# Pooled attention with a gated convolution layer: narrower waits for the second product, one operation for the values' low parts, a new written order

## The chip, the cores and the metric

The kernel runs on one core of one Trainium2 chip. The metric is the device time of one execution in microseconds (us), as the median of several runs. The engines of a core are named as the profile names them: PE is TensorE (PEld its weight loads), DVE is VectorE, ACT is ScalarE, POOL is GpSimd, SP is SyncE, which issues the DMAs here. They run side by side and wait for each other by semaphores.

## The reference, cut to what matters

```python
# q, k, v: (4 batches, 8 heads, 1152, 64) float32
q_pool = q.reshape(B, H, S // 2, 2, D).mean(axis=3)          # 576 queries
scores = np.matmul(q_pool, k.transpose(0, 1, 3, 2)) / np.sqrt(D)
scores = scores - np.max(scores, axis=-1, keepdims=True)
attn = np.exp(scores)
attn = attn / (np.sum(attn, axis=-1, keepdims=True) + 1e-09)
x = np.matmul(attn, v)        # -> (4, 576, 512), heads side by side
h = np.maximum(x @ w_in, 0.0)                                # 512 -> 1024
conv_out = sum(conv_w[k] * hp[:, k:k + S, :] for k in range(3))   # along the tokens
gate = 1.0 / (1.0 + np.exp(-conv_out))
out = (h * gate) @ w_out                                     # 1024 -> 512
```

The weights come as float64 and are turned to float32 in the kernel.

## The kernel before, in words

The program is a list of tasks, each a few instructions on one engine. The functions `loads`, `softmax`, `values`, `scales`, `feed`, `second`, `weights`, `split`, `split_out` and `halves` add 2485 tasks to a `Plan`, with an engine, a planned duration, the tasks that must come before (`after`), and the buffers that it takes and uses. A search made elsewhere has written down its result as three strings: ORDER (the order in which all tasks are emitted), SLOTS (which buffer of its ring each task takes) and SWAPPED (which tasks run on their other engine). `order()` unpacks them; the last loop of the kernel emits the tasks one by one. Every engine works through its own instructions strictly in that order, and a wait arises wherever an instruction touches a buffer that another engine or a DMA still writes or reads.

The 32 heads are worked in 16 pairs. For each pair `loads` brings keys, queries and values in, sums the two query halves and, where a head's values are split, makes a high and a low fp16 part (`hi_v`, and `lo_v` at L408, one VectorE operation for each head). `softmax` goes over five tiles of 128 queries (the last has 64 of each head): scores on PE (L468) into one of two score buffers, the maximum on VectorE (L481), the exponential on ScalarE (L486), the row totals (L499 or L503) and their inverse (L509), then either a high and a low fp16 part (L529 or L534, then L537) and a DMA transpose, or for the heads in the set X32 a normalisation (L570 or L574), transposes on PE (L588) and their eviction (L597 or L599). `values` multiplies (L620, L626) and evicts (L638 or L642, then L646 or L648 and L653).

When the four pairs of a batch have a group of query tiles ready, `feed` makes the first product in eight blocks of 128 features (L715), relu (L722 or L726), three convolution taps (L733 or L737, L744), tanh (L750) and the gate (L754). `second` then makes the second product of each of the five token tiles in four steps of two feature blocks (`mm2`: L928 for the halved groups in fp16, L934 in float32, L940 for the short last tile), evicts it (L954) and stores it (L960, L963). A tile at the end of a group needs one more column from the next group, the edge (L895, L902, L915). `weights` turns the float64 weights (L1017 to L1050); `split` and `split_out` split them into halves.

Matmuls use the array in four tile shapes: 64x128 for scores (row tiles), 64x64 for the last query tile's scores, 128x64 for values and the short token tile, and 128x128 for the rest. SP's queue issues all loads, DMA transposes and stores in the written order, too. The keys' ring has four buffers, the queries' and values' input rings have one each, the outputs' two.

Of the kernel before, what the change touches and what calls it, by code (L numbers as in the profile page):

```python
# [13 lines left out]
ALU = mybir.AluOpType  # L14
# [74 lines left out]
def unpack(words):  # L89
# [10 lines left out]
bcjykia9kekckkjzkfkdkjkaj8bGklkgbabdkzkbdQbekmbfkMbgj9kndxkokAkpd4kwd5bhkBkxkUkCbidykykDbjkHkskVkXktkNkEbkkWkq  # L100
kYkukreokFblkZlckvbmkGk0lfk1dzk9ldk2kKd8bnk3kLdLlgkIk4bwkJdBlebok5dCdDk7dElafHlhlubplbk6lxlik8d9ealjbHlrkQlklv
ebdAbsdFlylwlsbqdGbIlzdHlMbrdKkRltlplAbxlPbJlqlBlNlJlClnllbKlolOlDlQbLdRlKl4bUlElmbylFl5bulRlLlHbtl6mplSlGlTms
mqlUdSd7lIbVl1dTlVmtl7lZlWl0dVbWdWlXl8ewl2mhmrbzdXl3bXmubYbAc3lYbBdYmvbZb0mHepmwd2mEmxmImib1myl9mCmKmFbMmDmjmz
mAmcmLmJmGjjmdmMmamZmBmNdZm2memOm0d0mPmbmWmfbNm3mQmgbOmRmUm1d1mSbPd6bCm4bQnhmXkOnkmTbRmYesmlbSeunim5bTmVedm6nl
njdUb2neevjknfeteenzbvngnmnMm7nAnnb3kSnommnpb4eJkPbDefb5nwmkb6nsnNnxntnaehnbnOeinBnyncb7nunPb8nUndd3nCejnvb9nX
nDnEnVnHm8ciDInYerm9nWeLnqekDJnrelnInFemDgnZDKenocnJmnn0eqcjn1ofDhn5eZn2odnGnKjnDunLn3oeD3DiogDvckexDwoaD4clob
Dxn6ohcmn8oucneMcooxn7ovcpeNnQn9oiD5eycaojoyokgtoweODjone0oln4moozkToMD6DLnRDkoPoAcboBoNoFoCosoqDyotnSoQoroGDz
ccoIoHegoJoDooDlDnopoOomDAeznTDBDoDmDMoRe2eBo4cdDCoED7oSDNDDoTeCoKoUo5oXDPoLeDceo6oYcfppDOD8cge3pspqchDQo7oZo2
o0oVo3cqprphDpeEo8pto9pcDEo1joe4papupdD9pbpipHDqcrDFpvpKpecspweFoWpxpIDReGpfDGEapypgpJpApLeIDWEbDHpMpBctpZDSeH
DXpCDrpDeKDYEhpNpEcue5EcpOcvpSpPp0pFp2DseApGcwplp3eQcxDtp4cyDZEifjpQpzDTp1EdEepXD0Efqzp5pmp6EgpYp7pTqApVpUqaqh  # L110
DUpWqBflqfqiqdqgqCD1qbDVqepRqkqDp8qcqEeRqHECqlqjEjeSp9qmqFqIqUqJqnD2qXczqoqVqpEDqKEoqsqYqWqLqqqGqvEpq8qwEqeTqZ
eUEkficAqtq9qrqxfnEErbq0ErqyfmEFqMq1Esq5q2rcraq6Etquq3rdrmq7eVqNcBrpreEGrfrnEHrgeWEQEurjq4rqEvERrkrrEXrhrorlcC
rArsEweYrDExrBESriqQrtcDrxrurEforyrFfAeXrCrve1rOqRrzElrGrHEIEmr5rLrPEYrIrXEyrQcEr6cFrRrMe7rwsjEZrYrJE4r7fDrSJQ
skr8rNEzrTEJr9EArUsaE5gArKE0slETsmsbEnscE1EKsgsdE6snrVE2ELsee8sArWe9soshE7fEEMsffFfaENsxEBspEOEUE3EVEPE8fbsqr1
sysufCsiEWszsrfgfGpjssFifUqOsBstePe6FarZFjsvsCFbqPsDJTsOsEfcr2fdsLsFswfWsIFcsMsPsNFkE9sJr3FdffsQsKfesZsGsRFefY
sSr4fksTfZs0sHFfsWs1sUtgFgsXfqtjfXths8sYs2tis3pks4tkFhFls5s9tlr0s6tafhtuFmtmtbtntxs7trtvfrpnFAfstwtytoFVFBtpFH
# [24 lines left out]
"""
SLOTS = (
    "01232301012301231010000010101000001000000002001111111002222203000004310000111340200222650000001001100112111120"
    "02240311002005212001121411002210510300000201200113110100221230300006021100001101001101012100010110211020113010"
    "03211010011000001100011120110010012100101103110210123002101103011011021312002001011131000102102002110331110010"
    "00122201140003110001111000110013012103111020311010010202001204102013100111100201011310013210112201211010031002"
    "00011120101000301110110201233201001210001110121113140311231100201220002113312111002003211113120110031002101211"
    "10203320301212021313121000220011110023120011302101000313221103110021100110211021110321102301000012311001110100"
    "14120022100131003110200022311100101223121213102201110001031220023121110030001300111300221101220010111003223032"
    "11130000010410131220112231100103132013120102000101230302110213201211010100100211022331321001011203011210022103"  # L150
    "22301011100001202311210231130012020401113021211002000103130120010031120103001100010000202011312312130000002130"
    "31311100020001011010013120300032021011130031311111121012013000001011110000023111211132100300021030121001131011"
    "2000300301113100211001021100100110"
)
SWAPPED = """
acalaqauaDaIaMaRaVa4bdbibobsbubybGbObWb4ccckcscAcPcQcScTcUc8dadmdsdvdGeaemeseOeWe2gogygHgYhIhKhQhThXh4h6ifiBiD
iQiZi9jijjjmjnjvjxjEjNjPjRjWj5kCkEkSlilAl1l7mmmnmvmPmWm5nennnpnCnOnSn0oiokonoAoSo7pjpnpvpPpSpWp7qpqCqOqSq0q2re
rgrjrsrurGrLrRrTrZr2sgspsrsusDsRsTsWs4tatetotrtAtCtOtQt2t4t7udufulupuxuRuWu7u9vcvrvEvQvUv4v7wgwiwlwuwzwIwNwVw0
w1w5xdxfxixrxtxwxFxHxKxTxVxYx4ycygyoyqytyCyEyHySyVy9zhznzrzvzFzRzTzWz5z7AjAoAuAwACAGAKASAUAXA6BbBkBmBpByBABJBR
BVBYBZB7CcClCqCzCBCECNCYC0C6DaDeDhDiDpDwDDDJDKDRDYD5EcEiEjEqExEEELESEZFCFJFQFXF4GbGiGpGwGDGKGRGYG5HcHWH2H3H9Ia  # L160
IhIoIvIBICIJIQIXI4JbJiJwJDJMJOJYJ0J4KFKMKTK0K7LeLlLsLBLDLHLOLVL2L9MgMnMuMDMFMJMPMQMXM3M4NaNbNhNiNpNw
"""
# [11 lines left out]
def tile_pooled_attention_conv_gate_ffn(  # L174
# [11 lines left out]
    B, H, S, D = Q_SHAPE  # L186
# [56 lines left out]
    def dve(n):  # L243
        return 0.115 + n / 930.0
# [1004 lines left out]
```

## Time and profile before

| what | us |
|---|---|
| median of 3 runs | 612.47 (611.01 to 613.85) |
| the profiled execution's own time | 611.83 |
| its span in the trace | 609.9 |
| PE busy in the span | 575.6 (94%) |
| DVE busy | 567.5 (93%) |
| ACT busy | 439.5 (72%) |
| POOL busy | 297.0 (49%) |

The span runs from the first to the last instruction of the trace; the 1.9 us that the execution's own time has beyond it lie before and after. A busy share is an average over stages, so the rows further down are taken by stage. The ends of matmuls are modelled, so PE's busy time holds pauses that don't show. DMA engines were busy with the core's transfers for most of the span, 83.6% of sixteen engines' time by the packets of the one large queue.

### The profile page before, as it was taken

The page shows a single profiled execution, that of the slowest core. Times are in us where ns is not written, and L with a number is a line of the kernel's source. Part 1 is how long each engine was busy: PE and PEld are TensorE (multiplying, and loading weights), DVE is VectorE, ACT ScalarE, POOL GpSimd, SP SyncE. Part 2 cuts the span into 40 slices and gives each one's busy share as a digit, 9 for nine tenths or more (in the row PEclk, how much of TensorE's full clock was granted, in tenths as well). Part 3 has the DMA queues.
Part 4 walks back from the last instruction along what each step waited for, and adds up shares of the span by engine and source line. Part 5 has one row for each costly group of instructions (what it writes and reads, how often), then busy time and mean ns, then how long its engine had stood idle before and what let it go on. Part 6 is the DMA issues. An engine that isn't in the chain of part 4 may idle for free.

```text
span 609.9 us, 11967 instructions
## 1 busy us (share of the span) xinstructions
PE 575.6 (94%) x4454; PEld 351.7 (58%) x4454; DVE 567.5 (93%) x921; ACT 439.5 (72%) x847; POOL 297.0 (49%) x306
## 2 busy tenths in 40 slices
PE   5989998789999999999998999999999999999997
PEld 2545554466665665556566665565557456675753
DVE  4999999999999999999999999999999999999871
ACT  4999998889998977676666876567556776574431
POOL 2353545558345536436645644655363445534630
PEclk9999989999999999999999999999999999999999
DMA  8454956977958699999999599998997999898701
GB/s 295 157 194 128 216 121 157 189 164 167 231 99 228 136 170 232 203 189 176 243 186 207 141 206 191 177 227 148 222 240 139 194 202 201 146 154 149 111 35 44
DMA packets 266713, 106.97 MB, mean 175 GB/s; under 512 B 254368, under 2 KB 255648, under 8 KB 266656
## 3 DMA queue, kind: packets, MB, share of 16 engines
q1 hardware_dynamic: 266656, 106.21, 83.6%
q8 instruction: 35, 0.57, 0.4%
q14 instruction: 22, 0.18, 0.1%
HBM read 37.77 MB, written 4.72 MB: 70 GB/s over the span
## 4 chain that ended last, share of the span: by engine, by line
PE 44%; DVE 27%; issue 5%; ACT 4%; POOL 2%; DMA 1%; SPq 0%; ACTq 0%; POOLq 0%; DVEq 0%
PE s L468 11%; PE a L715 10%; DVE hl L537 9%; DVE sm L481 8%; PE a L934 7%; PE a L620 7%; DVE g L744 4%; PE a L928 3%; PE a L626 2%; PE a L588 2%; DVE g L754 1%; ACT p L486 1%; PE a L940 1%; POOL hl L529 1%; DVE v L408 1%
## 5 line engine op out<-in xcount | busy, mean ns | idle before, releaser
L486 ACT ACTIVATE p<-s,sm 128x1152 f32<-128x1152 f32 x144 | 175.3, 1219 | 64.1 <-DVE sm L481 42.0
L481 DVE TENSOR_REDUCE sm<-s 128x1 f32<-128x1152 f32 x144 | 193.1, 1347 | 11.3 <-PE s L468 9.7
L468 PE MATMUL s<-kt,qt 64*128 64x128 f32 (+2 forms) x704 | 182.4, 474 | 11.1 <-ACT p L486 6.3
L537 DVE SCALAR_TENSOR_TENSOR hl<-p,sm,hl 128x1152 f16<-128x1152 f32 (+1 forms) x111 | 161.9, 1468 | 2.7 <-POOL hl L529 1.4
L529 POOL TENSOR_SCALAR hl<-p,sm 128x1152 f16<-128x1152 f32 (+1 forms) x72 | 96.6, 1346 | 107.9 <-DVE sm L509 76.3
L468 PE MATMUL s<-kt,qd 64*128 64x512 f32 x256 | 145.4, 650 | 1.7 <-DMA kt<-in_k_dram 1.7
L620 PE MATMUL a<-pt,v 128*64 128x256 f16 (+2 forms) x1512 | 111.6, 271 | 1.3 <-ACT h L726 1.1
L468 PEld LDWEIGHTS s<-kt,qt 64*128 64x128 f32 (+1 forms) x704 | 78.6, 176 | 58.9 <-ACT p L486 24.8
L715 PE MATMUL a<-x,wi 128*128 128x257 f16 (+3 forms) x864 | 104.6, 274 | 2.4 <-ACT o L954 1.1
L620 PEld LDWEIGHTS <-v 128*64 128x64 f16 x1512 | 86.9, 110 | 20.2 <-issue 16.1
L715 PEld LDWEIGHTS <-wi 128*128 128x128 f16 x864 | 77.4, 98 | 36.7 <-issue 18.4
L737 POOL TENSOR_SCALAR g<-h,cw 128x255 f32<-128x255 f32 (+3 forms) x70 | 50.8, 730 | 61.2 <-ACT h L726 40.5
L934 PE MATMUL a<-wo,g 128*128 128x512 f32 x160 | 75.4, 605 | 0.0
L744 DVE SCALAR_TENSOR_TENSOR g<-h,cw,g 128x255 f32<-128x255 f32 (+3 forms) x144 | 73.4, 529 | 1.5 <-POOL g L737 1.1
L588 PEld LDWEIGHTS a<-ident,p 128*128 128x128 f32 (+1 forms) x360 | 37.3, 142 | 49.4 <-issue 11.9
L588 PE MATMUL a<-ident,p 128*128 128x128 f32 (+1 forms) x360 | 53.9, 278 | 12.3 <-ACT pt L597 6.5
L626 PE MATMUL a<-pt,v 128*64 128x256 f32 (+1 forms) x288 | 64.1, 408 | 0.0
L574 POOL TENSOR_SCALAR p<-p,sm 128x1152 f32<-128x1152 f32 (+1 forms) x31 | 41.6, 1344 | 44.1 <-DVE sm L509 41.2
L534 ACT ACTIVATE hl<-p,sm 128x1152 f16<-128x1152 f32 (+1 forms) x39 | 48.7, 1250 | 9.1 <-DVE sm L509 7.8
L934 PEld LDWEIGHTS a<-wo,g 128*128 128x128 f32 x160 | 28.1, 190 | 38.2 <-issue 35.9
L597 ACT ACTIVATE pt<-a 128x384 f32<-128x384 f32 (+2 forms) x100 | 45.4, 473 | 6.1 <-PE a L588 5.5
L726 ACT ACTIVATE h<-a,bs 128x257 f32<-128x257 f32 (+3 forms) x62 | 29.8, 483 | 25.6 <-PE a L715 14.3
(137 smaller groups left out, 661.9 us busy)
## 6 DMA issues: line engine op xcount, KB each, us to landing
qin<-in_q_dram SPq DMA_DIRECT2D x15, 640.0 KB, 4.7
kt<-in_k_dram SPq DMA_DIRECT2D x15, 576.0 KB, 5.1
vin<-in_v_dram SPq DMA_DIRECT2D x9, 576.0 KB, 4.6
g<-in_moe_w_in_dram SPq DMA_DIRECT2D x8, 512.0 KB, 4.4
w<-in_moe_w_out_dram SPq DMA_DIRECT2D x8, 512.0 KB, 3.7
out_dram<-o SPq DMA_DIRECT2D x16, 256.0 KB, 3.1
pt<-hl SPq DMA_TRANSPOSE x120, 4.9
vin<-in_v_dram SPq DMA_DIRECT2D x6, 288.0 KB, 3.0
```

What stands on the lines that cost most here:

```text
L468: nc.tensor.matmul(out=w, lhsT=f, rhs=kk, start=True, stop=True)
L481: nc.vector.tensor_reduce(out=sm[:, e:e + 1], in_=runs(st[e]), axis=AX.XY, op=ALU.max, negate=True)
L486: nc.scalar.activation(out=p.tile().rearrange("p (a n) -> p a n", a=2), in_=runs(st[e]), func=AF.Exp, bias=sm[:, e:e + 1], scale=1.0, accu ...
L529: eng.tensor_scalar(out=hl[rows, 0], in0=ps_[e][rows], scalar1=sm[rows, 6 + e:7 + e], scalar2=1.0, op0=ALU.mult, op1=ALU.mult,)
L537: nc.vector.scalar_tensor_tensor(out=hl[rows, 1], in0=ps_[e][rows], scalar=sm[rows, 6 + e:7 + e], in1=hl[rows, 0], op0=ALU.mult, op1=ALU.s ...
L588: nc.tensor.transpose(w[:, (i - a1) * nq:(i - a1 + 1) * nq], ps_[e][rows, i * P:(i + 1) * P], ident[rows, rows])
L620: nc.tensor.matmul(out=to, lhsT=o.v[:, e, c, vc:vc + D], rhs=o.pt[y, e][:, hl * NC + c, 0:n], start=(c == 0 and j == 0), stop=(c == NC - 1 ...
L626: nc.tensor.matmul(out=to, lhsT=o.v[:, e, c].bitcast(F32), rhs=p32.rearrange("p (a n) -> p a n", a=NC)[:, c, 0:n], start=(c == 0), stop=(c ...
L715: nc.tensor.matmul(out=w[:, 0:n], lhsT=wi[:, a, j, f * P:(f + 1) * P], rhs=x.x[:, c, s0:s0 + n], start=(i == 0 and j == 0), stop=(i == 2 a ...
L737: eng.tensor_scalar(out=g[:, f % 4, 0:tok], in0=h[:, 0:tok], scalar1=cw[:, f, 0:1], scalar2=1.0, op0=ALU.mult, op1=ALU.mult,)
L744: nc.vector.scalar_tensor_tensor(out=c, in0=h[:, t:t + tok], scalar=cw[:, f, t:t + 1], in1=c, op0=ALU.mult, op1=ALU.add)
L934: nc.tensor.matmul(out=w.tile(), lhsT=g[f // 4][:, f % 4, c:c + P], rhs=wo[:, f, :], start=(f == 0), stop=(f == FC - 1),)
```

## The change

Three things. `lo_v` takes both heads of a pair in one VectorE operation where both are split (nine of the sixteen pairs), so there are 2476 tasks. In `second` and `split_out` the `after` lists get narrower: a step names only its own two gates, its own edge column and its own blocks of `w_out`, instead of all eight. And ORDER, SLOTS and SWAPPED are new: the search was run again from there.

```diff
 ORDER = """
-cIcGaacJcMcOcNcPcHhCc6asabcKaccLhDdoc7hFbEadhEcQcTaecRcSafhYhGatauhHagcYcUahhZhIcXh1cWcVhJhKh0c5hRh2hNaihLavhO
+cIcGaacMcOcNcPcHhtcJcKasabachucYhwadcQaecRhvafcThxcShPaghycUahhzhScXhAcWhBcVhQaic5cLathIaBhEhThRc4auhLhMavhFaw
...
 SLOTS = (
-    "01232301012301231010000010101000001000000002001111111002222203000004310000111340200222650000001001100112111120"
+    "01232301012301230010000010101000001000000011002111103001222200000005310100211640200122451300000000000112211110"
...
 SWAPPED = """
-acalaqauaDaIaMaRaVa4bdbibobsbubybGbObWb4ccckcscAcPcQcScTcUc8dadmdsdvdGeaemeseOeWe2gogygHgYhIhKhQhThXh4h6ifiBiD
+acahalauazaIaVa4bdbobubybGbObWb9ccckcscAcOcTcUcWdbdmdsdudMdPeveGeOeWfcgChzhDhHh6iaihipisiDiJiQiWjajejmjojujvjE
...
-        def lo_v(e):
+        def lo_v():
             nc.vector.scalar_tensor_tensor(
-                out=o.v[:, e, :, D:P], in0=o.vin[:, e], scalar=o.vs[:, 5:6], in1=o.v[:, e, :, 0:D],
-                op0=ALU.mult, op1=ALU.subtract,
+                out=o.v[:, es, :, D:P].rearrange("p e c d -> p (e c) d"),
+                in0=o.vin[:, es].rearrange("p e c d -> p (e c d)"), scalar=o.vs[:, 5:6],
+                in1=o.v[:, es, :, 0:D].rearrange("p e c d -> p (e c) d"), op0=ALU.mult, op1=ALU.subtract,
             )
...
-        o.vls += [
-            add("DVE", dve(576), lambda e=e: lo_v(e), after=[t], uses=[o.vs, o.vin, o.v], port=True)
-            for e in two
-        ]
+        o.vls.append(add("DVE", dve(n), lo_v, after=[t], uses=[o.vs, o.vin, o.v], port=True))
...
-            sums.append(add("ACT", act(2 * DM, 0.12), total, after=wo_ready, takes=[bufs[j]]))
+            sums.append(add("ACT", act(2 * DM, 0.12), total, after=wo_ready[2 * j:2 * j + 2], takes=[bufs[j]]))
...
-        g, need = gs[u], list(done[u])
+        g, need = gs[u], [done[u][2 * i:2 * i + 2] for i in range(4)]
...
-            need = [[hr[0]], [hr[1]]]
+            need = [[hr[i // 2]] for i in range(4)]
...
-            need += [add("POOL", 0.25, lambda i=i: edge(i), port=True, after=done[u] + done[u + 1],
-                         uses=[g[i], gs[u + 1][i]]) for i in range(2)]
+            for i in range(2):
+                e = add("POOL", 0.25, lambda i=i: edge(i), port=True, uses=[g[i], gs[u + 1][i]],
+                        after=done[u][4 * i:4 * i + 4] + done[u + 1][4 * i:4 * i + 4])
+                need[2 * i:2 * i + 2] = [[e], [e]]
...
-                last = [add("PE", 1.3, lambda i=i: mm2(i), after=need[i // 2] + last + wh[2],
+                last = [add("PE", 1.3, lambda i=i: mm2(i), after=need[i] + last + wh[2][i:i + 1],
                             uses=gh + wh[0] + ([w] if i else []), takes=[] if i else [w])]
...
-                        after=need + last + wo_ready, uses=g + ([w] if i else []), takes=[] if i else [w])]
+                        after=need[i] + last + wo_ready[2 * i:2 * i + 2], uses=g + ([w] if i else []), takes=[] if i else [w])]
```

## Rows read from the trace of the kernel before

**Rows 1.** Busy us (and count) by stretch: start:end, length, then each engine.
```profile
core 0: us, PE busy (x) PEld busy (x) DVE busy (x) ACT busy (x) POOL busy (x), PEclk, DMA share, GB/s
0.00:30.00 30.00, 21.95 (x93) 12.31 (x95) 21.05 (x37) 21.54 (x42) 9.95 (x16) 1.00 0.65 230
30.00:90.00 60.00, 54.70 (x390) 32.23 (x388) 58.37 (x99) 56.42 (x110) 30.18 (x32) 0.97 0.65 168
90.00:210.00 120.00, 110.26 (x827) 69.50 (x825) 115.36 (x191) 107.03 (x205) 64.88 (x64) 1.00 0.77 173
210.00:450.00 240.00, 236.77 (x1719) 142.59 (x1716) 234.10 (x355) 165.20 (x298) 122.58 (x115) 1.00 1.00 194
450.00:570.00 120.00, 117.06 (x1094) 74.37 (x1094) 116.06 (x178) 77.06 (x159) 57.85 (x58) 1.00 0.95 170
570.00:612.00 42.00, 34.89 (x355) 20.72 (x348) 22.52 (x67) 12.27 (x37) 11.55 (x23) 0.99 0.21 53
```

**Rows 2.** VectorE's waits from 30 to 570 us: us in total, times, longest.
```profile
DVE sm L481 <- PE s L468: 5.6, 13, 0.8
DVE hl L537 <- POOL hl L529: 1.4, 2, 1.1
...
```

**Rows 3.** The chain that ended last, its end: start us, length, what.
```profile
594.54 7.77 PE a L928 x36
602.31 3.63 PE a L940 x32
...
606.01 0.38 ACT o L954
```

**Rows 4.** The values' low parts by line (xcount, busy us, mean ns), and two chain pieces.
```profile
L408 DVE SCALAR_TENSOR_TENSOR v<-vin,vs,v 128x576 f16<-128x576 f32 x24 | 19.5, 820 | 0.0
...
350.65 2.66 DVE hl L537 x2
...
360.23 1.46 DVE v L408 x2
```

**Rows 5.** VectorE's kinds that are exchanged, by line and shape: busy us, mean ns.
```profile
L599 DVE COPY pt<-a 128x384 f32<-128x384 f32 x11 | 5.9, 552 | 0.3 <-PE a L588 0.2
L1030 DVE TENSOR_SCALAR wo<-g 128x512 int32<-128x512 int32 x8 | 3.4, 430 | 0.6 <-POOL g L1021 0.6
L305 DVE TENSOR_TENSOR qin<-qin 128x640 f32<-128x640 f32 x4 | 3.3, 818 | 0.0
L503 DVE SCALAR_TENSOR_TENSOR sm<-sm,small 128x2 f32<-128x2 f32 x17 | 2.6, 152 | 0.1
L574 DVE TENSOR_SCALAR p<-p,sm 128x1152 f32<-128x1152 f32 x3 | 2.4, 815 | 0.0
L722 DVE TENSOR_SCALAR h<-a,bs 128x257 f32<-128x257 f32 x5 | 2.4, 477 | 0.0
L638 DVE TENSOR_SCALAR xf<-a,vs 128x320 f32<-128x320 f32 x2 | 1.1, 538 | 0.2 <-issue 0.2
```

**Rows 6.** ScalarE's high part of softmax, by line and shape.
```profile
L534 ACT ACTIVATE hl<-p,sm 128x1152 f16<-128x1152 f32 x34 | 42.4, 1250 | 8.9 <-DVE sm L509 7.8 <-ACT xf L642 0.5 <-ACT pt L597 0.4
```

**Rows 7.** The chain, TensorE's pieces around 240 us (x10: two score tasks).
```profile
237.01 1.28 PE s L468 x5
...
240.05 1.72 PE a L934 x4
...
243.05 1.91 PE a L934 x4
...
256.95 2.14 PE s L468 x10
```

**Rows 8.** The keys' loads (L264): time from issue to landing.
```profile
DMA to landing us min/median/max: 3.2/5.1/8.5
```

More of the change, by code (lines that the diff above doesn't have):

```diff
@@ L100 @@
[L100 to L104, printed above, removed]
@@ new lines @@
+j9dgjZjIbdkbj0a8kabedqj3a9kcj1j4kqdNbfkddPkDj6d5bakedxbgj7kfkrknkgbhkskokLj2bwktdybiklkMkEkOkmd8kpkudzkNkjkPkh
+bjkyk3kQbkkkkvkBk4bxkik6kRkCkSkwk0blkzkTbmkAkxbnk5dBdCk7fnkWewbybokYkXbsdDkUdEk1llk8dFk2lmdGealokVk9ebdHkHbqla
+lplbdKlibpd9ljlqbHkZlkbrlnlclDbIkIlrldlsbJlAltlelEd7lgdIlGlhdQlBlFludRbKlVlHlfbLdSlwlvlWlIbubUlyd4epdTlxlXlCmg
+btlJlzlKlYlLlSdVmhmjbVdWbWlOmklMlPlNlQdXlTl8mibzbXmlbAlZdYbBbYdZbZmmlUd0mnmvb0dAmyd2mol0mwlRl9mpb1mBmzmqmamtbM
+mCmAmrl3mud1mQmDl1d6msl6mEl7l4mFmRl2mNmGmTl5mSjamxmLmUesmJmKbNmHjbmOm8mVbOmMm9nbmIkFedmPbPetmckGbQeud3bRmWbSmX
@@ new lines @@
+ncbTm5nabCdUm6b2mYnqndm7mbevm3mdbvm4m1nem2nDnfnrnnb3eJngerb4ecb5eenob6nsnhefb7nLb8nEnteLninjnMnFmZnknOm0menunv
+nGbDb9ehDznyeinNcinPnpnlkJDAejnwn3nQDBnBeknmeln6eNDCemnRnCnSn4nTnWnzC7nAnxcjn7DUckC8n5clnUDlDVC9cmnZDmDan0nXn8
+Dnn1cnolDbeneMooDDn2eqeOn9DWnVoaomoenHobDooncoopcpexeZDcoceycanYDdoqodojDXoDDpDYnIorosokofoEowotohoGezoiouogDq
+eBozcbeCovoAeDoxccoHDZDsoye1oFDecdegoIjeeEDrjfoVDfceoJDtoKD0DEDGkKoOoLoWoBDHDueFoCcfoToXnJoPDvpgoMoQpjoYoUeGoZ
+pho3o0oRo8cgpiDgDwchpkoSe3DIcqplDhnKDio4o9eHpye4o1o5eKpBDjoNDFo6pmmfDNo7pnpzpoprD1DODkpCpAo2psD2pppQcrptD3Dxpq
@@ new lines @@
+pupRpDcsD8DPD4pveQctpwD5pTcupxeIDypEpSDJeYpcpFpUpGe2D6DKfhcvfgDLDQpJpHD9DMpVDRD7pMcwqqpWpNcxpXpdpYpKqrpOp1cypL
+p8pIpPqsfjp6p9p4p7qbqtp5qupZqvp2Etqyqcp3p0qaqweRqdqLeSEuqeqzqfeTqMqgqjqOqAeAqhczqBEfqNEaqPqiEvqCqZcAEgeUEbqQEh
+cBqmq0qkfQq2qlqxqnEwDSEcqoqRqDqSq3qWqTeVq4DTqUqpqXq1rdqVEiq5flrgq6Exq7EdreEHraq8qYqEEIEmrhEyEJrfEjEOEzq9ricCcD
+fmrbrufkrrrjEPrkcErceWrlqHrsrorvfxEQrprwrmrtrFeXrnrxEkqIrWryElrCrzrGEVEne0fArXEorqrHrOrArIEKrYrDrBrZfCELrPsaEp
+EMrJr0rKEArEEer1cFsbEWEBePERr2fDrLe6sdfzESrNENe7EXr3e8r7r4serMfBfEe5e9E9ECETr8scfaEYEqr5ErsfsoEDr6EEsrEsEFsgEZ
@@ L141 @@
+NZ
 """
 SLOTS = (
[L143 to L147 removed]
@@ L162 @@
+rzrIrKrQrUr2r4sislsuswszsKsTsVs1s5tftrtwtHtKtTtYt4ucuguouGuIuPuRu0u7vivvvHvLvTvVvYv7v9wlwnwqwzwBwEwKwMwSwWw4w6
+w9xkxnxwxyxBxKxMxPxVxXx6x7yfykytyyyHyJyMy0y6y8zezizmzuzwzIzNzWzYAaAfAtAxAAABAJALAOAXAZBgBpBrBABIBMBQBYB0CcCeCh
+CqCsCECPCXC0C1C5DgDnDuDBDIDPD3EaEhEvECEJEQFtFAFGFHFOFVF2F9GgGnGuGBGIGPGWG3HaHNHUH1H7H8IfIlImItIzIAIHIOIVI2I9Jg
+JnJuJDJFJTJVKwKDKKKRKYK5LcLjLsLuLyLFLMLTL0L7MeMlMuMwMAMGMHMNMOMVM2M9NfNgNmNn
 """
@@ L910, in second @@
                             uses=[gh[i], gs[u + 1][i]])
-                    need.append([add("DVE", 0.13, lambda i=i: edge_low(i), port=True, after=[e],
-                                     uses=[gh[i], gs[u + 1][i]])])
+                    need += 2 * [[add("DVE", 0.13, lambda i=i: edge_low(i), port=True, after=[e],
+                                      uses=[gh[i], gs[u + 1][i]])]]
         elif t == groups[u][-1] and u < len(groups) - 1:
```

91 lines of the change are left out of this document (40 added, 51 removed).

## The prediction

> **What bounds the kernel now.** I read the busy times by stage first [rows 1]. In each stretch the reader should subtract a column from the length. VectorE (DVE) leaves 1.6 us of 60 free from 30 to 90 us, 4.6 of 120 from 90 to 210, 5.9 of 240 from 210 to 450 and 3.9 of 120 from 450 to 570: 16.0 us in 540, so it is 97% busy all through. TensorE (PE) leaves 5.3, 9.7, 3.2 and 2.9 us in the same stretches: it has air until 210 us and almost none after. ScalarE is nearly full until 90 us and falls to 64 to 69% after 210 us; GpSimd is about half full. The granted clock is 1.00, the 2.4 GHz level, in nearly every row, so clock is no term here. So this is a VectorE bound with TensorE close behind, and the two ends are different: the first 30 us cost VectorE 9.0 us of waiting for the first data, and in the last 42 us VectorE has only 22.5 us to do while TensorE has 34.9.
>
> Second I read what VectorE waits for between 30 and 570 us [rows 2]: the largest entry is the scores, 5.6 us in 13 waits; the next is 1.4 us. Nothing there is a single stall worth removing. Third, the chain that ended last, at its end [rows 3]: from 594.54 to 605.94 us it is TensorE alone, 7.77 us of second-product matmuls and 3.63 us of the short last tile, then one eviction and the store. The span ends at 609.9; the run's own time is 611.83, 1.9 us more. That run lies 0.6 us under the median of 612.47, and I move my sum by that.
>
> **What the change is, once it is decoded.** The `after` lists of a task are read by nothing that emits code: `order()` takes the written ORDER, SLOTS and SWAPPED, and the loop emits task by task. So the narrowed waits of `second` and `split_out` change no instruction themselves; they only permit other orders. I decoded both strings and compared the two lists of tasks. Of the 80 steps of the second product, two (tile 2 of batch 0) stand before the last gate of their group in the new order, and none in the old. So the headline change is hardly used, and I give it zero. What it costs if I am wrong: those two steps stand in a stretch where VectorE sets the pace. The rest is a new order, new buffers and some engines exchanged.
>
> **VectorE's work.** (a) The values' low parts: 9 of 16 pairs have two heads in fp16, so nine pairs of 576-column operations become nine of 1152. Two in a row took 1.46 us in the chain; the 1152-column operation of the same form took 2.66/2 = 1.33 us [rows 4]. That is 0.13 us each, 1.2 us in all; by the mean durations, 2 x 820 ns against 1330, it would be 2.8 us, and the lower end is 0. I take 1.2, since the two chain rows are measured start to start. The high part before it already covers both heads, so no new wait arises; a short operation queued behind it may come 0.6 us later. The Trainium skill, "VectorE: DVE Perf Modes", section on the TRN2 errata, gives a fixed 58 cycles per SBUF-to-SBUF operation: as an estimate 60 ns each at 0.96 GHz, 0.5 us for nine. The rows show twice that, and the sum uses the rows.
>
> (b) Exchanged engines. Onto VectorE: 7 more transposed blocks kept (0.552 us each, 3.86; one of them is narrower) and 3 clamps of weights (no row on VectorE; the nearest are 512 columns at 430 ns, 1.29 in all, and 257 at 477 ns, 1.43; I take the first, of the same width; 0 if they replace a wait). Off VectorE: 2 value evictions (0.538, 1.08), 2 relus (0.477, 0.95), 3 query sums (two of 640 columns at 0.818, one of 384, scaled to 0.49: 2.13), one normalisation (0.815) and 3 row totals (0.152, 0.46) [rows 5]. Net -0.3 us. With (a): VectorE's work falls by 1.5 us, bounds 0 to 3.5. At 97% busy nearly all of that is on the path.
>
> (c) ScalarE takes 7 more high parts of softmax at 1.25 us [rows 6] and gives away the seven blocks: some 8 us more in all, most of it after 140 us of VectorE work where ScalarE has a third of its time free [rows 1]: 0. GpSimd loses work: 0.
>
> **TensorE's order.** I counted how often neighbours in its queue use different tile shapes of the array (128x128, 64x128 for scores, 128x64 for values and the short tile, 64x64): 225 times before, 246 after. The chain shows the price [rows 7]. Ten score matmul records in a row take 2.14 us, so five cost 1.07; five alone, before another kind, take 1.28: 0.21 us for leaving. Four records of the second product take 1.72 us after a first product and 1.91 us after scores: 0.19 us for entering. I use 0.19 per change. Of the 21 more, 10 fall before the 54th score task of 144, some 200 us in, where TensorE has 15.0 us of air behind the first 30 us: 0, and up to 1.9 if that air sits elsewhere. Six fall from there to the last score, where TensorE has 6.1 us free and VectorE is as full: up to 1.1, I take 0.5. Five fall after the last score, where TensorE alone sets the end [rows 3]: 5 x 0.19 = 0.95, taken whole. The Trainium skill, "TensorEngine Tiling (Array Packing)", section on tiling modes, says that a switch of tiling mode drains TensorE; that speaks against this order, and the 0.21 and 0.19 agree with it.
>
> **Score buffers.** There are two. A score task that takes the buffer of the one just before it must wait until ScalarE has read that one. In the written orders 17 tasks do so before and 11 after. VectorE's 5.6 us of waits on scores [rows 2] are the nearest row: 6/17 of it is 2.0 us, the lower bound is 0; I take 1.5, since all that waiting sits at scores.
>
> **SP's queue.** The keys of pair 3 are issued much later: in the written order 5.0 us of VectorE work lies between the issue and the first use, where 57 lay before; the keys of pairs 5 and 10 go early instead. Such a load lands after 3.2 to 8.5 us, 5.1 in the median [rows 8]. TensorE's queue stops at that score task; behind it stand the next score and transposes, and VectorE's next maximum waits for it. Cost 0 to 3.5 us, by the row's middle near nothing: 0.3. Other loads keep margins of at least the old minimum (about 3.5 us).
>
> **The very end.** The last tile is now a full one instead of the short one: a wider eviction (0.38 us now [rows 3]) against one store issue fewer. 0, bounds -0.5 to +0.5.
>
> **Sum.** -1.5 (VectorE) + 0.95 (shapes at the end) + 0.5 (shapes before) - 1.5 (score buffers) + 0.3 (keys) = -1.25 us. From 611.83 that is 610.6 on the profile's run; from the median 612.47, **611.2 us**.
>
> **Rivals.**
> 1. *The new order fills VectorE's gaps.* Its 16.0 us between 30 and 570 us are small gaps, and a new order can lose or keep them. If the waits on scores go whole, 5.6 instead of 1.5, and a sixth of the start's 9.0 us with the earlier second half of the first keys: 611.2 - 4.1 - 1.5 = 605.6. For it: the fewer repeated buffers, and the first keys' second half is issued one place earlier. Against it: I set the engines' work side by side at each 20 to 60 us of VectorE work, and the two orders differ by under 3 us of TensorE work anywhere.
> 2. *Slower: TensorE's shape changes decide.* If TensorE, not VectorE, sets the pace from 210 us on, the 11 changes behind the 54th score count with leaving and entering, 0.40 us: 4.4 us in place of my 1.45, 614.2. What VectorE then saves there saves nothing: the low parts (all of pairs 6 to 15) give back 1.2 and the buffers 1.5: 616.9. Its point: TensorE has 6.1 us free from 210 to 570 us now; 11 changes at 0.40 eat 4.4 of them, and from there on each further change is paid in full. For it: VectorE has more free there, 9.8 us. Against it: VectorE's waits on TensorE in all of 30 to 570 us are 5.6 us, so most of that free time is not TensorE's doing. The Trainium skill's rule of the drain (the section named above) would speak for this rival.
> 3. *The keys of pair 3 come late*, at the slow end of the row: 3.5 us in place of 0.3: 614.4. That is still within 0.5%.
> 4. *It does not do what it says*: if nothing but the low parts matters, 612.47 - 1.2 = 611.3, the forecast's own time.
>
> **How the numbers follow.** A measurement of this kernel tells some 0.5% from no change, 3.1 us. Forecast together with rival 4: 0.44, within 0.5%. Rival 1: 0.32, faster. Rival 2: 0.16, slower. Rival 3: 0.08, of which 0.06 within and 0.02 slower. So faster 0.32, same 0.50, slower 0.18. The range reaches to rival 1 and rival 2: 605.5 to 617. With the bounds of the unknown costs (VectorE 0 to 3.5, shapes 0.95 to 4, buffers 0 to 2, keys 0 to 3.5) the forecast's own range is 608 to 615.
>
> **What would show it.** In the profile after: VectorE's busy total near 566 us with nine low parts of 1152 columns near 1.33 us start to start, and DVE's waits on scores between 30 and 570 us near 4 us. TensorE's last stretch without gaps, a little longer than before from the last first-product task to the end. Wrong if VectorE's free time between 30 and 570 us moves by over 4 us either way (the order, not the work, then sets the time), if TensorE's share of the chain after 210 us grows at its cost, or if a wait of over 1.5 us on pair 3's keys stands near 85 us.

## The result and the profile after

The changed kernel takes 606.62 us in the median of six runs (606.17 to 607.22), the kernel before 611.74 (610.24 to 613.85, six runs beside it). The ratio is 0.9916, 95% interval 0.9893 to 0.9938: 5.1 us faster. That lies in the range, near its lower end, but it is not the forecast's 1.25 us; by its size it is the first rival. Lines between some L410 and L886 have moved up by two in the new kernel: scores L466, maximum L479, exponential L484, low part of softmax L535.

Busy time by stretch of the changed kernel, to be set beside [rows 1] (same columns):

```profile
0.00:30.00 30.00, 21.99 (x99) 11.88 (x101) 21.74 (x38) 21.22 (x44) 10.58 (x18) 1.00 0.71 252
30.00:90.00 60.00, 55.10 (x392) 31.13 (x390) 57.33 (x96) 56.46 (x112) 32.15 (x32) 1.00 0.61 142
90.00:210.00 120.00, 112.16 (x825) 69.50 (x827) 115.93 (x193) 108.01 (x204) 59.50 (x61) 0.99 0.80 175
210.00:450.00 240.00, 237.60 (x1717) 143.51 (x1714) 232.28 (x347) 169.43 (x305) 120.10 (x118) 1.00 1.01 202
450.00:570.00 120.00, 118.45 (x1143) 77.34 (x1141) 117.08 (x182) 82.47 (x166) 51.28 (x56) 1.00 0.96 169
570.00:612.00 42.00, 30.86 (x292) 16.30 (x289) 18.65 (x60) 8.66 (x26) 9.00 (x18) 0.97 0.08 29
```

Subtract PE's column from the lengths between 30 and 570 us: TensorE leaves 16.7 us free, where it left 21.2. Subtract DVE's: 17.4 free, where it was 16.1. So it is TensorE's free time that shrank, and VectorE's did not. TensorE's matmuls are the same number, 4454, and their busy sum over the span hardly moved, 575.6 us before and 576.2 after. One could stop at VectorE's total, which fell from 567.5 to 563.0 us; the experiments below show that this total does not carry the time.

VectorE's waits from 30 to 570 us, as in [rows 2]:

```profile
DVE sm L479 <- PE s L466: 6.7, 14, 2.0
DVE g L742 <- POOL g L735: 1.6, 4, 0.4
DVE hl L535 <- POOL hl L527: 1.5, 2, 1.1
```

The wait on scores did not fall, it was 5.6. The rows that did move are on the two other engines of the same loop. A score buffer goes round in it: TensorE writes the scores, VectorE takes the maximum, ScalarE the exponential, and then TensorE may write that buffer again. TensorE has two queues in the profile, the matmuls (PE) and the weight loads (PEld), which run ahead of them. The first view is of the score line and says what ended the idle time ahead of it, on both queues added up (us, times; 30 to 570 us). The kernel before:

```profile
its engine sat idle before it (us, times) until:
  ACT p L486: 27.5, 48
  issue: 19.5, 60
```

and the changed kernel:

```profile
its engine sat idle before it (us, times) until:
  ACT p L484: 19.5, 41
  issue: 16.8, 58
```

The matmul queue alone waited for exponentials ahead of scores (us in total, times, longest), first before and then after:

```profile
PE s L468 <- ACT p L486: 5.3, 10, 1.4
```

```profile
PE s L466 <- ACT p L484: 2.5, 7, 0.7
```

The rest of the 27.5 and 19.5 us is the weight loads'. The row can't be read as time in which TensorE stands still: 27.5 us are more than the 21.2 that its matmuls leave free. Of the weight loads' 22.3 us before, some 5 fall in time in which no matmul runs; in the others earlier matmuls still run. What the matmuls themselves waited less is 2.8 us, of the 4.5 by which their free time fell.

The next view is what ScalarE waited for in the same time, first before and then after:

```profile
ACT p L486 <- DVE sm L481: 40.6, 30, 4.3
```

```profile
ACT p L484 <- DVE sm L479: 23.1, 22, 3.1
```

Exponentials wait 17.5 us less for their maxima, and TensorE's two queues together wait 8.0 us less until an exponential frees a buffer. By stretch TensorE's row went from 3.6 to 2.8 us (30 to 90 us), 11.5 to 7.3 (90 to 210), 7.8 to 3.5 (210 to 450) and 4.7 to 5.9 (450 to 570). Of ScalarE's 17.5 us, 16.1 lie between 210 and 450 us, where ScalarE has time to spare. One wait of the weight loads outside this loop grew, the transposes' for ScalarE's evictions: 9.8 us before, 14.6 after.

The end of the chain, beside [rows 3]:

```profile
590.69 2.59 PE a L928 x12
593.28 2.74 PE a L940 x24
596.02 1.40 PE a L928 x6
597.42 1.01 PE a L940 x8
598.44 2.71 PE a L928 x12
601.17 0.69 ACT o L954
```

TensorE alone again, now mixing the two tile shapes, and a wider last eviction: 0.69 us where it was 0.38.

### The profile page after: what moved, and what is told of

It is laid out like the page before. It is cut to its first block, busy times and chain, and to the rows that moved or that the text cites. A ratio compares the mean times of both kernels' runs of the same rounds, so it can differ in the third digit from the quotient of the medians.

```text
span 604.8 us, 11969 instructions
## 1 busy us (share of the span) xinstructions
PE 576.2 (95%) x4454; PEld 349.7 (58%) x4454; DVE 563.0 (93%) x911; ACT 446.3 (74%) x854; POOL 282.6 (47%) x300
## 4 chain that ended last, share of the span: by engine, by line
PE 38%; DVE 15%; issue 4%; ACT 4%; POOL 3%; DMA 2%; SPq 0%; POOLq 0%; DVEq 0%; ACTq 0%
PE s L466 9%; PE a L934 8%; PE a L618 7%; PE a L713 7%; DVE hl L535 6%; DVE sm L479 4%; PE a L928 3%; DVE g L742 3%; POOL hl L527 2%; DMA pt<-hl 2%; PE a L940 2%; ACT p L484 1%; PE a L624 1%; DVE g L752 1%; PE a L586 1%
## 5 line engine op out<-in xcount | busy, mean ns | idle before, releaser
L484 ACT ACTIVATE p<-s,sm 128x1152 f32<-128x1152 f32 x144 | 175.3, 1218 | 57.2 <-DVE sm L479 24.2
L479 DVE TENSOR_REDUCE sm<-s 128x1 f32<-128x1152 f32 x144 | 193.1, 1346 | 10.8 <-PE s L466 10.4
L466 PE MATMUL s<-kt,qt 64*128 64x128 f32 (+2 forms) x704 | 183.1, 473 | 8.5 <-DMA kt<-in_k_dram 5.0
L535 DVE SCALAR_TENSOR_TENSOR hl<-p,sm,hl 128x1152 f16<-128x1152 f32 (+1 forms) x111 | 160.6, 1453 | 2.2 <-POOL hl L527 1.5
L527 POOL TENSOR_SCALAR hl<-p,sm 128x1152 f16<-128x1152 f32 (+1 forms) x65 | 85.7, 1322 | 129.0 <-DVE sm L507 82.0
L466 PE MATMUL s<-kt,qd 64*128 64x512 f32 x256 | 144.6, 647 | 1.0 <-DMA kt<-in_k_dram 1.0
L466 PEld LDWEIGHTS s<-kt,qt 64*128 64x128 f32 (+1 forms) x704 | 77.3, 175 | 51.3 <-ACT p L484 20.9
L742 DVE SCALAR_TENSOR_TENSOR g<-h,cw,g 128x255 f32<-128x255 f32 (+3 forms) x144 | 70.9, 512 | 4.3 <-POOL g L735 3.9
L532 ACT ACTIVATE hl<-p,sm 128x1152 f16<-128x1152 f32 (+1 forms) x46 | 57.6, 1252 | 15.8 <-DVE sm L507 8.1
L572 POOL TENSOR_SCALAR p<-p,sm 128x1152 f32<-128x1152 f32 (+1 forms) x32 | 43.6, 1363 | 49.5 <-DVE sm L507 39.0
L586 PE MATMUL a<-ident,p 128*128 128x128 f32 (+1 forms) x360 | 55.4, 277 | 10.9 <-ACT pt L595 7.0
L595 ACT ACTIVATE pt<-a 128x384 f32<-128x384 f32 (+2 forms) x93 | 42.5, 474 | 6.4 <-PE a L586 6.2
```

Source lines behind the costliest of these rows:

```text
L466: nc.tensor.matmul(out=w, lhsT=f, rhs=kk, start=True, stop=True)
L479: nc.vector.tensor_reduce(out=sm[:, e:e + 1], in_=runs(st[e]), axis=AX.XY, op=ALU.max, negate=True)
L484: nc.scalar.activation(out=p.tile().rearrange("p (a n) -> p a n", a=2), in_=runs(st[e]), func=AF.Exp, bias=sm[:, e:e + 1], scale=1.0, accu ...
L527: eng.tensor_scalar(out=hl[rows, 0], in0=ps_[e][rows], scalar1=sm[rows, 6 + e:7 + e], scalar2=1.0, op0=ALU.mult, op1=ALU.mult,)
L532: nc.scalar.activation(out=hl[rows, 0], in_=ps_[e][rows], func=AF.Copy, scale=sm[rows, 6 + e:7 + e])
L535: nc.vector.scalar_tensor_tensor(out=hl[rows, 1], in0=ps_[e][rows], scalar=sm[rows, 6 + e:7 + e], in1=hl[rows, 0], op0=ALU.mult, op1=ALU.s ...
```

## The experiments

All ratios are to the kernel before, measured beside it. Where two programs differ by a written string, the first line of the string that differs stands in the diff. Times are medians; one profiled execution can lie 2 us and more from its kernel's median (24 executions of the kernel before in one set went from 608.2 to 614.7), so spans are not compared below 4 us.

**1. The joined low parts alone.** Order, buffers and engines are the old ones.

```diff
-        o.vls += [add("DVE", dve(576), lambda e=e: lo_v(e), after=[t], uses=[o.vs, o.vin, o.v], port=True)
-            for e in two]
+        o.vls.append(add("DVE", dve(n), lo_v, after=[t], uses=[o.vs, o.vin, o.v], port=True))
```

> The old order, buffers and engines; only the values' low parts of nine pairs joined, nine VectorE operations fewer. Theory A (VectorE's work sets the time): VectorE's busy total falls by 1.0 to 1.5 us and the time with it, a ratio of 0.998 to the kernel before. Rival B (the new order as a whole does it, by filling gaps): the joined operations are hidden, ratio 1.000. Rival C (a longer VectorE operation delays short ones queued behind it): ratio above 1.000.

612.42 us, ratio 1.0019 [1.0001, 1.0037]: no gain, if anything a loss of 1 us.

**2. The changed kernel with the low parts apart.** Each joined task is two tasks again, one behind the other.

```diff
-        o.vls.append(add("DVE", dve(n), lo_v, after=[t], uses=[o.vs, o.vin, o.v], port=True))
+        o.vls += [add("DVE", dve(576), lambda e=e: lo_v(e), after=[t], uses=[o.vs, o.vin, o.v], port=True)
+            for e in two]
```

> The new order, buffers and engines, with the low parts of each head apart again, one right behind the other. Theory A: 1.0 to 1.5 us slower than the changed kernel, 0.994 of the kernel before in place of 0.9916. Rival B: no change, 0.992. If the whole gain hung on the joined operations: 1.000.

605.94 us, ratio 0.9926 [0.9907, 0.9946]. The whole gain is there without the joined operation. The page of this run:

```profile
PE 577.1 (95%) x4454; PEld 348.0 (58%) x4454; DVE 566.4 (94%) x920; ACT 446.6 (74%) x854; POOL 284.0 (47%) x300
```

VectorE is busy 566.4 us, only 1.1 less than in the kernel before and 3.4 more than in the changed one, and the time is the changed kernel's. So VectorE's busy total is not what the gain is made of.

**3 and 4. The exchanged engines without the rest, and the rest without them.** 166 tasks stand on another engine in the new string. Experiment 3 puts it into the kernel before, experiment 4 the old one into the changed kernel.

```diff
 SWAPPED = """
-acalaqauaDaIaMaRaVa4bdbibobsbubybGbObWb4ccckcscAcPcQcScTcUc8dadmdsdvdGeaemeseOeWe2gogygHgYhIhKhQhThXh4h6ifiBiD
+acahalauazaIaVa4bdbobubybGbObWb9ccckcscAcOcTcUcWdbdmdsdudMdPeveGeOeWfcgChzhDhHh6iaihipisiDiJiQiWjajejmjojujvjE
```

> The old order and buffers with the new choice of engines (325 exchanged tasks become the new 313). Theory A by work alone: VectorE loses 0.3 us by the sum of rows, GpSimd 14 us, ScalarE gains 7: ratio 0.997 to 1.000, with VectorE's operations held up less by GpSimd. Rival B (order and engines only fit each other): the order written for other engines lets tasks queue behind each other, ratio 1.00 to 1.02.

634.75 us, ratio 1.0386 [1.0354, 1.0418].

> The new order and buffers and the joined low parts with the old choice of engines. Theory A by work alone: 0.3 us more on VectorE and more GpSimd work beside it: ratio 0.992 to 0.996. Rival B: the order loses its fit and with it the gain, 1.00 to 1.02.

636.28 us, ratio 1.0420 [1.0398, 1.0442]. Either half alone costs some 4%. A sum of engine times, as I made it, sees nothing of this: it priced the exchange at -0.3 us.

**5. The changed kernel with the old arrangement of its last steps**, the full tile ahead of the short one.

```diff
 ORDER = """
...
-NcMxNHMYM5MMNNMINKM6MNMOMPNlMJMQMKNdNLMRMSMLMZNmNQNeNMNfNRNgNnNhNUNiNONoNpNjNPNqNkNrN0NINSNTN1N2NVN3NWN4N5NXNY
-NZ
+NcMxNHMYM5MMNNMINKM6MNMOMPNlMJMQMKNdNLMRMSMLMZNmNQNeNMNfNRNgNnNhNUNiNONoNpNjNPNqNkNrNINSNTNVNWNXNYNZN0N1N2N3N4
+N5
```

> The changed kernel, but at the end the full tile 3 is finished first and the short tile 4 last, as before: four changes of tile shape on TensorE fewer, and the last store is the short tile's. If the arrangement of the end gave some of the gain (VectorE's end to the span's end is 12.6 us before and 10.8 after): up to 1.5 us slower, 0.994. If the shape changes cost 0.19 us each as the prediction had it: 0.8 us faster, 0.990. If TensorE's backlog alone decides, with the same matmuls: 0.9916, and from the last first-product task to TensorE's end the same time within 0.3 us.

606.56 us, ratio 0.9922 [0.9894, 0.9949]: the very end is worth nothing that can be measured, as the prediction had it.

**6. More work for ScalarE.** 56 first taps of batches 1 to 3 go from GpSimd to ScalarE in the changed kernel: SWAPPED loses their tasks.

```diff
 SWAPPED = """
...
-CqCsCECPCXC0C1C5DgDnDuDBDIDPD3EaEhEvECEJEQFtFAFGFHFOFVF2F9GgGnGuGBGIGPGWG3HaHNHUH1H7H8IfIlImItIzIAIHIOIVI2I9Jg
+CqCsCECPCXC0C1C5DgDnDuDBDIDPD3EaEhEvECEJEQFGH7IlIzJDJFJTJVLsLuMuMwMGMNNfNm
...
```

> The changed kernel with the first convolution tap of batches 1 to 3 (56 operations of 0.3 to 0.85 us) on ScalarE in place of GpSimd. Theory D (VectorE's operations with two inputs are held up when a GpSimd operation has just begun; in the changed kernel those behind a first tap lose some 3.6 us): VectorE's busy total falls by 2 to 3 us and the time by 1 to 3, ratio 0.987 to 0.990. Rival: ScalarE, 26 us fuller, delays the exponentials behind it and VectorE waits: ratio above 0.992.

613.17 us, ratio 1.0035 [1.0018, 1.0052]. ScalarE is busy 468.2 us in place of 446.3, GpSimd 248.2 in place of 282.6, and VectorE 565.4 in place of 563.0, so taking GpSimd's work away did not shorten VectorE's. TensorE's row ahead of scores (both queues, 30 to 570 us, here and in all that follow):

```profile
its engine sat idle before it (us, times) until:
  ACT p L483: 30.4, 56
```

ScalarE's free third, which I had priced at nothing, is not free: 21.9 us more on it cost 7.3 us against the changed kernel (0.0119 of 611). The row, 10.9 us longer, says that exponentials come later; that they queue behind the taps is the likely reason and not shown by itself.

**7. The kernel before with its two score buffers strictly in turn**, so that no score task takes the buffer of the one just before it (17 did). Only the digits of score buffers in SLOTS differ, 88 of them. The string is broken into lines of 110 digits in the one kernel and 108 in the other, so the lines don't start at the same digit; the lines shown hold the first digit that differs, the 263rd.

```diff
 SLOTS = (
...
-    "03211010011000001100011120110010012100101103110210123002101103011011021312002001011131000102102002110331110010"
...
+    "301003211010011000001100011120110010012100101113100210123002101103111011021302012001011031100102002102110330"
...
```

> The kernel before with the two score buffers strictly in turn in the written order, so that no score task takes the buffer of the one just before it (17 did). The prediction's term: VectorE's waits on scores fall, 5.6 us at most, ratio 0.994 to 0.998. Rival: the buffer that was used earlier is not the one that comes free first, ratio 1.000 or above.

625.02 us, ratio 1.0221 [1.0196, 1.0246].

```profile
its engine sat idle before it (us, times) until:
  ACT p L486: 49.9, 60
```

22.4 us more in that row and 13.5 us more time (0.0221 of 611), 0.60 us for each us of the row. Counting successions is refuted as a measure: their number went to none, and the waits went up.

**8. The changed kernel with the old `after` lists.** The program is the same, instruction by instruction; only line numbers differ.

```diff
-                last = [add("PE", 1.3, lambda i=i: mm2(i), after=need[i] + last + wh[2][i:i + 1],
+                last = [add("PE", 1.3, lambda i=i: mm2(i), after=need[i // 2] + last + wh[2],
...
-                        after=need[i] + last + wo_ready[2 * i:2 * i + 2], uses=g + ([w] if i else []), takes=[] if i else [w])]
+                        after=need + last + wo_ready, uses=g + ([w] if i else []), takes=[] if i else [w])]
```

> The changed kernel with the planner's lists of predecessors for the second product, its edge columns and the sums over w_out as before; order, buffers, engines and joined low parts new. Theory A: these lists emit nothing, the program is the same, ratio 0.9916 within its interval. Rival (the narrower waits act in the program): up to 1.000.

606.40 us, ratio 0.9918 [0.9885, 0.9950]. The narrowed lists change nothing by themselves.

The next four take work away from one engine at a time, or change the buffers in the new order. Theories A, B and C: VectorE's work sets the pace, the loop of the score buffers sets it, TensorE's work sets it.

**9. The kernel before with shorter maxima.**

```diff
-        def runs(t):
-            f = t[:, 0:HS]
-            return bass.AP(f.tensor, f.offset, [list(f.ap[0]), [RUN, 2], [1, HS]])
+        def runs(t, n=HS):
+            f = t[:, 0:n]
+            return bass.AP(f.tensor, f.offset, [list(f.ap[0]), [RUN, 2], [1, n]])
...
-                    out=sm[:, e:e + 1], in_=runs(st[e]), axis=AX.XY, op=ALU.max, negate=True
+                    out=sm[:, e:e + 1], in_=runs(st[e], HS - 32), axis=AX.XY, op=ALU.max, negate=True
```

> The kernel before, with each of the 144 maxima of scores over 1088 of its 1152 columns (the softmax needs no exact maximum). At 1347 ns for 1152 columns, 64 fewer take up to 75 ns off each, some 10 us of VectorE's work, and they lie in the loop in which a score buffer comes free: maximum, exponential, next score. Theory A (my prediction's): VectorE's work sets the pace, 97% busy, so the time falls by 9 to 10 us, ratio 0.983 to 0.986. Theory B: the loop through the two score buffers sets it. TensorE's idle time ahead of score matmuls that ends with ScalarE's exponential is 27.5 us in the kernel before, 19.5 in the changed one and 49.9 with the buffers in turn; shorter maxima shorten that loop, so that this row falls by 5 to 10 us and the time as much, ratio 0.983 to 0.992, more than the same cut on the taps. Theory C: TensorE's own work sets it: under 3 us, ratio above 0.995.

610.48 us against 610.15, ratio 1.0010 [0.9992, 1.0027]. The groups of VectorE by line show the cut (busy us, mean ns | idle before):

```profile
L481 DVE TENSOR_REDUCE sm<-s 128x1 f32<-128x1088 f32 x144 | 183.7, 1281 | 13.5 <-PE s L468 12.3
```

193.1 us became 183.7, and nothing came of it. VectorE's waits on scores went from 5.6 us in 13 to 9.2 in 24, its other instructions took 3.2 us longer in sum (561.3 = 567.5 - 9.4 + 3.2), and TensorE's row stayed, 28.5. Theory A is refuted, and so is B as I had put it, with its 5 to 10 us. C's "under 3 us" held.

**10. The kernel before with shorter taps**, outside the loop.

```diff
-                c = g[:, f % 4, 0:tok]
+                k = tok - 64 if tok > 200 else tok
+                c = g[:, f % 4, 0:k]
                 nc.vector.scalar_tensor_tensor(
-                    out=c, in0=h[:, t:t + tok], scalar=cw[:, f, t:t + 1], in1=c, op0=ALU.mult, op1=ALU.add
+                    out=c, in0=h[:, t:t + k], scalar=cw[:, f, t:t + 1], in1=c, op0=ALU.mult, op1=ALU.add
```

> The kernel before, with 64 fewer columns in each of the 128 wide taps of the convolution on VectorE; those columns lack taps 1 and 2 (left out). By the rows, (533 - 287) ns over 190 columns, 64 columns are 83 ns, 10.6 us of VectorE's work in all, outside the loop of the score buffers, from about 90 to 590 us. Theory A: VectorE's work sets the pace, so the time falls by 9 to 10.6 us, ratio 0.983 to 0.986, as with the shorter maxima. Theory B: taps only delay the maxima that are queued behind them; about half is taken up by waits: 4 to 6 us, ratio 0.990 to 0.994. Theory C: ratio above 0.996.

609.05 us against 610.15, ratio 0.9981 [0.9966, 0.9996]: 8.7 us off the taps (73.4 to 64.7 by line) bring 1.2 us. Most of the rest went into VectorE's gaps, which grew from 29.8 to 36.3 us up to its last instruction. A's 9 to 10.6 us and B's 4 to 6 are refuted; C's ratio above 0.996 held.

**11. The kernel before with fewer value products** on TensorE.

```diff
                 for j, (hl, vc) in enumerate(((0, 0), (0, D), (1, 0))):
                     for e in range(2):
                         to = w[D * e:D * e + D, 0:n]
                         if not o.x32[e]:
+                            if j == 2 and c % 9 in (1, 3, 5, 7):
+                                continue
```

> The kernel before, without four ninths of the products of the probabilities' low parts with the values (192 of the 432 fp16 chunks' third matmul, left out). In the chain 54 such matmuls in a row took 3.07 us, 57 ns each, so that TensorE has 10.9 us less to do, spread over the whole kernel. Theory A: VectorE sets the pace and TensorE only at the end: 0 to 2 us, ratio 0.997 to 1.000. Theory B: TensorE comes earlier to score tasks that wait for their buffer, and that idle row grows from 27.5 us by most of the 10.9; 2 to 4 us, ratio 0.993 to 0.997. Theory C: TensorE's work sets the pace, 9 to 11 us, ratio 0.982 to 0.986.

It left out 224 of 504 such matmuls, not 192 of 432, and PE's busy sum fell by 5.2 us, not 10.9: 23 ns for each, not 57. Why so little is not shown. 608.62 us against 610.15, ratio 0.9960 [0.9938, 0.9981], 2.4 us.

```profile
its engine sat idle before it (us, times) until:
  ACT p L486: 36.8, 60
```

The row grew by 9.3 us, and TensorE's free time over the span grew from 34.3 to 37.4 us: over half of what the matmuls were spared they spent waiting. C is refuted at its 9 to 11 us, and B's 2 to 4 us held in number; but both were worked out for 10.9 us less work, and there were 5.2. Of these nearly half reached the time, against none of 9.4 us and 1.2 of 8.7 us on VectorE. So of the three cuts the one on TensorE counted most.

**12. The changed kernel with the old choice of score buffers**, 55 digits of SLOTS. Again the lines shown hold the first digit that differs, the 263rd.

```diff
 SLOTS = (
...
-    "03210011100001110100111120000110112100100113200200123101020103110011121302211011011030120102002112010331100110"
...
+    "310103210011100001110100111120000110112100100103210200123001120103010011121312201011011130020102102012010331"
...
```

> The changed kernel, in which each score task takes the buffer that it takes in the kernel before (55 of 144 differ); order, engines and everything else are the new ones. A score task takes the buffer of the one just before it 19 times (11 in the changed kernel, 17 before). By my prediction's price, some 0.25 us for each such task, 2 us are lost: ratio to the kernel before 0.995. If the choice of buffers belongs to its order, as the kernel before with buffers in turn showed (2.2% for none in succession), the idle row before scores grows from 19.5 us by 10 or more, and the gain is gone: ratio 1.01 to 1.03.

630.39 us, ratio 1.0315 [1.0283, 1.0347]: 24 us more than the changed kernel.

```profile
its engine sat idle before it (us, times) until:
  ACT p L484: 58.2, 59
```

38.7 us more in the row for 24.3 us of time (0.0399 of 610), 0.63 each. With the same order and the same engines, the choice of 55 buffers decides over four times the gain. Not all of it is waiting: the granted clock is 0.97 from 330 to 570 us, where the changed kernel has 1.00, and the same matmuls are busy 9.6 us longer.

The rows of the loop in all kernels, 30 to 570 us: idle time of TensorE's two queues ahead of scores until an exponential, ScalarE's wait for maxima, VectorE's wait for scores.

| kernel | ratio | TensorE, us | ScalarE, us | VectorE, us |
|---|---|---|---|---|
| before | 1 | 27.5 | 40.6 | 5.6 |
| 1, low parts joined | 1.0019 | 31.0 | 39.9 | 6.6 |
| 9, shorter maxima | 1.0010 | 28.5 | 35.1 | 9.2 |
| 10, shorter taps | 0.9981 | 26.8 | 35.5 | 7.6 |
| 11, fewer value products | 0.9960 | 36.8 | 41.3 | 5.1 |
| 7, buffers in turn | 1.0221 | 49.9 | 37.9 | 17.4 |
| 3, new engines in the old order | 1.0386 | 40.6 | 45.5 | 8.2 |
| changed | 0.9916 | 19.5 | 23.1 | 6.7 |
| 2, low parts apart | 0.9926 | 22.3 | 27.3 | 4.2 |
| 5, old last steps | 0.9922 | 20.1 | 27.1 | 6.3 |
| 8, old `after` lists | 0.9918 | 20.9 | 25.5 | 4.2 |
| 6, taps on ScalarE | 1.0035 | 30.4 | 21.6 | 7.3 |
| 4, old engines in the new order | 1.0420 | 38.1 | 27.2 | 5.7 |
| 12, old score buffers | 1.0315 | 58.2 | 22.3 | 26.0 |

The four programs whose time is within 0.2% of the kernel before have 26.8 to 31.0 us in the TensorE column, the four whose time is the changed kernel's 19.5 to 22.3: the difference is not the accident of one execution. ScalarE's column does not go with the time: it is as low in 4, 6 and 12, which are slower than the kernel before.

At the 0.60 to 0.63 us for each us of the row that experiments 7 and 12 give, which change buffers and nothing else, the 8.0 us from the kernel before to the changed one are worth 4.8 to 5.0 us; measured were 5.1. This is a fit and not a test. The price comes from losses of 13 and 24 us, and part of these is the clock's: the mean granted clock of the runs was 0.986 to 0.992 in 7 and 0.981 to 0.989 in 12, against 0.988 to 1.000 in the kernel before beside them. Without the 9.6 us of longer matmuls the price from 12 is 0.38, and the 8.0 us are worth 3.0. By the matmuls' own waits (5.3 to 16.0 us in 7, 2.5 to 21.0 in 12) each us costs 1.3, and their 2.8 us are worth some 3.6. All of these are estimates from the rows named.

Nor does the row price everything: in 11 it grew while the time fell, since there TensorE had less to do, and in 3 and 4 the time grew by more, PE's busy sum being 5.8 us longer in 3 and 7.9 us longer in 4 than in its own base.

## Why the prediction was right and wrong

The time lies in the range because the range was wide: its lower end was set by rival 1, and the forecast's own range, 608 to 615 us, misses 606.62. The outcome, faster by 0.8%, had been given a chance of 0.32.

**The bound, the first step, failed.** I called it "a VectorE bound with TensorE close behind" from a busy share of 97%. Experiments 9 and 10 took 9.4 and 8.7 us off VectorE and got 0 and 1.2 us; 5.2 us off TensorE got 2.4. So TensorE was nearer to setting the time than VectorE, and neither sets it alone. Each engine works strictly in the written order, and in these runs what one was spared it spent in good part waiting for another.

**The narrowed lists at zero** held, by experiment 8.

**VectorE's work, -1.5 us.** As work it was sized well: the lines of joined and exchanged operations sum to some -1.8 us. (VectorE's busy total fell by 4.5 us, to 563.0 where 566 was forecast; the rest lies in operations that did not change in number, the taps' -2.5 us above all.) The joined operation has this group in the changed kernel:

```profile
L408 DVE SCALAR_TENSOR_TENSOR v<-vin,vs,v 128x1152 f16<-128x1152 f32 x9 | 13.1, 1455 | 0.0
```

1455 ns in the mean, not 1330, for 2 x 820: 185 ns less than two, where I took 130. As time it was wrong: joining moved nothing in experiment 1, and parting nothing in 2. "At 97% busy nearly all of that is on the path" is the sentence that failed. The Trainium skill, "VectorE: DVE Perf Modes", section on the TRN2 errata, states a fixed 58 cycles for each operation in its table, and below it that the measured term is about 150. As estimates these are 60 and 156 ns for each joined pair; the trace's 185 ns are nearer to the second. In time no run here can tell either from 0.

**ScalarE at zero** was right for the changed kernel's few us in their places, but not as a rule: experiment 6.

**Shape changes, +1.45 us.** Not to be seen: PE's busy sum went up by 0.6 us with 21 more changes, its free time went down, and the time fell. No run tests this term alone. Rival 2, which made it decide, gave 616.9 us and is out: TensorE's free time from 210 to 570 us is 4.0 us now, in place of the 6.1 of its point, and yet the kernel is faster. That a switch of tiling mode drains TensorE, as the Trainium skill states ("TensorEngine Tiling (Array Packing)", section on tiling modes), may hold; its price in time is not shown here.

**Score buffers, -1.5 us.** This is the term that was mis-sized, and the likely carrier of the result. I priced it from VectorE's waits on scores, 5.6 us, as "the nearest row", and bounded it by 2.0; that row did not fall, it is 6.7 now. The same loop makes TensorE wait ahead of its score line, 27.5 us on its two queues and 5.3 of them on the matmuls, and I did not read that row. It fell by 8.0, and the matmuls' part by 2.8. That buffers can move the time by far more than 2.0 us is shown by experiments 7 and 12 (13.5 and 24.3 us); that they, and not the rest of the order, brought the 5.1 is not. Its measure, successions in one buffer, was wrong as well: none of them cost 13.5 us more in the old order (experiment 7).

**Keys of pair 3, +0.3 us, and rival 3.** No wait on keys stands after the first 30 us in the changed kernel; there are two of them, 6.0 us, at the start (6.5 before). The margin of 5.0 us was enough.

**Rival 1** had the size, 605.6, and half of the mechanism: the order fills gaps. The size is luck in part, for it placed the gaps on VectorE, whose gaps did not shrink (16.1 to 17.4 us), and gave the start 1.5 us, where nothing was gained. The 18th maximum begins at 68.9 and 68.0 us in the kernel before and in experiment 1, and at 67.8 to 69.8 in the changed kernel and its variants 2, 5 and 8: no gain yet. The 126th begins at 481.6 in both of the first and at 473.0 to 478.0 in the four: the gain grows between the two. My criterion for being wrong, VectorE's free time moving by over 4 us, looked at the wrong engine and did not fire: it moved by 1.3.

**What stays open** is which moves in the order shorten TensorE's waits ahead of the scores, and whether these waits are all of the gain. Order, buffers and engines were fitted to each other, and experiments 3, 4, 7 and 12 show that a part changed alone costs 2 to 4%; so the gain can't be divided among the three. Several engines made shorter at once, which would show whether the loop then yields, was not tried.

## What to carry to other kernels

Where several engines run a loop through few buffers in a written order, a busy share of 97% does not say that this engine's work sets the time: before pricing work, read what each engine of the loop waits for, above all the one that must stop until a buffer comes free. And see on which of an engine's queues a wait stands: weight loads that wait behind running matmuls may cost nothing. A new order, its buffers and its engines are one thing; read the waits along the loop beside the sums of work, test them together, and don't expect a part of them to bring its part of the gain.

## What the runs showed of the hardware

VectorE operations with two inputs in SBUF can last longer when they begin while a GpSimd operation runs. In the changed kernel one low part of softmax lay so (timeline: start, length):

```profile
472.19 2.52 POOL L527 TENSOR_SCALAR hl<-p,sm 128x1152 f16<-128x1152 f32 x2 [0.82 <-DVE sm L507]
473.61 2.31 DVE L535 SCALAR_TENSOR_TENSOR hl<-p,sm,hl 128x1152 f16<-128x1152 f32 x1
```

It took 2.31 us, where the line's median is 1.41, and ended 1.2 us after the second of GpSimd's two operations. The line as a whole (min/median/max ns):

```profile
L535 DVE SCALAR_TENSOR_TENSOR hl<-p,sm,hl x111: 1397/1409/2310, 47.0 to 560.6; 128x1152 f16<-128x1152 f32 x105, 64x1152 f16<-64x1152 f32 x6
```

Of the 105 full ones, 28 began while a GpSimd operation ran; none of the other 77 took over 1.42 us. The Trainium skill, "SBUF — State Buffer", section "Who interferes with whom", states that such an operation contends with a GpSimd operation that reads SBUF, and that the order of issue decides which of the two blocks; the trace agrees in this pair, where VectorE's came later. It is not shown to be where the gain is from: with 34.4 us of GpSimd's work gone, in experiment 6, VectorE's busy time did not fall.
